# The order of the experts in an attention, expert-routing and two-layer kernel: the two small experts move from the middle to the last step

## The chip, the cores and the metric

The kernel runs on one core of a Trainium2 chip. The metric is the device time of one execution in microseconds, and the median of several executions is quoted. TensorE (PE) does the matrix products, VectorE (DVE) and ScalarE (ACT) the elementwise work, GpSimd (POOL) issues the indirect transfers, SyncE (SP) issues all the others. Each engine works through its own queue in the order in which the program was written. They meet at semaphores.

## The reference, cut to what matters

Three layers follow each other: attention in a window of 64 positions, a layer of eight experts of which each token uses one, and a two-layer network that all tokens use.

```python
def _attn_ref(q, k, v):                      # 2 x 8 heads x 576 positions x 64
    scores = np.where(mask, scale * q @ k.T, -1e9)      # mask: 0 <= i - j < 64
    attn = softmax(scores)
    return attn @ v                          # as x: 1152 tokens x 512

def _moe_ref(x, w_gate, w1, w2, capacity):   # 8 experts, 512 -> 1024 -> 512
    logits = x @ w_gate
    expert_idx = np.argmax(logits, axis=1)
    ...
    h = np.maximum(np.einsum('ecd,edf->ecf', disp, w1), 0.0)
    y = np.einsum('ecf,efd->ecd', h, w2)
    out[i] = gate_w[i] * y[expert_idx[i], pos[i]]

def _moe2_ref(x, w_in, w_out, alpha):        # 512 -> 2048 -> 512
    h = x @ w_in
    g = np.maximum(h, 0.0) + alpha * np.minimum(h, 0.0)
    return g @ w_out
```

How many tokens an expert gets is known only when the router has run. The inputs are of type float32.

## The kernel before, in words

**Attention and routing** take the first 78 us. The experts are then ranked by how many tokens they have, rank 0 the largest. Eight positions p = 0 to 7 follow each other, and the table ORDER says which rank stands at which position. `room` gives each position a size: ranks 1 to 3 are **wide** (256 tokens), ranks 0, 4 and 5 **narrow** (128; the first 128 tokens of rank 0 have been done ahead in the attention phase), and ranks 6 and 7 are the **pair** (64 tokens each). What doesn't fit goes to a rare second pass.

**Weights.** An expert has eight chunks of 512 KB: four of its first matrix, four of its second. `stream` is the order in which the chunks are loaded. SP loads a chunk into a raw slot as soon as one is free (`load_on`, L110). There are 14 slots in this phase; only five of them may hold chunks of the network behind the experts (L115). A chunk of a wide or narrow expert is **split** into a rounded part `whi` (ACT L1017, every fourth on DVE) and the rest `wlo` (DVE L144); the split frees the raw slot and fills one of seven ring places. `prepare` writes these splits into the queues up to seven chunks ahead of the product that uses them. The pair is not split: its products read the raw chunks, which keep their slots until then.

**Products.** A wide expert computes in `wide_up` four times 24 matmuls of 256 columns (tile `hps`, L1033), after each of which ACT and DVE make `hh` (L1041) and `hl` (L1042), and in `wide_down` 96 matmuls (tile `y`, line 220, written by `mm3`) into four accumulators y0 to y3 for the four quarters d of the model's width. `put` turns each of them into the columns `x2h` (ACT L1059) and `x2l` (DVE L1060) that the network reads. A narrow expert does `sps`, `stp`, `sy` likewise, and its result is transposed (`ytp`) inside the next expert, as an entry of the list `late`. `ready` transposes the next expert's tokens (`xtp`, L1008) and splits them into `xwh` and `xwl` (L1093, L1094) for a wide, `xth` and `xtl` for a narrow one.

**The pair** runs as a generator inside the expert at position HOST: `pair()` transposes the pair's tokens, copies them on DVE to `xp` (L1171), and yields; then four times `pps` (L1189) with a yield after each, then four times `py` (L1205). `wide_up` and `wide_down` call it between their own chunks, by `between(c)`. Its result goes through `done` (ytp, then two pairs of ACT L1222 and DVE L1223), again by `late`.

**The network behind the experts** (`second_mlp`) computes `gps` (L220) and `ops` (L1326) in four rounds. Its weights come as 64-bit numbers, and `cvt_tick` makes float32 of them and splits them: per half chunk ACT L166 and L189, DVE L173, L174, L177 and L190. Four ticks stand inside the expert at position 7, which is wide: two in `wide_up` (after c = 2 and c = 3), two in `wide_down`, beside put(0) and put(1). Its first matmuls read all four quarters of x2 one after the other, quarter d in matmuls 3d to 3d + 2.

Before the change ORDER is (0, 1, 4, 5, 2, 6, 7, 3) and HOST is 4: narrow, wide, narrow, narrow, wide with the pair in it, wide.

Of the kernel before, what the change touches and what calls it, by code (L numbers as in the profile page):

```python
# [27 lines left out]
def attention_moe_mlp_kernel(  # L28
# [13 lines left out]
    nc = tc.nc  # L42
    B, S = 2, 576
    NE, NT, D = 8, 1152, 512
# [5 lines left out]

    ORDER = (0, 1, 4, 5, 2, 6, 7, 3)
    HOST, PAIR = 4, (5, 6)
    WIDE, NARROW, HALF = min(cap, 256), 128, 64
    room = [WIDE if 1 <= r <= 3 else HALF if r >= 6 else NARROW for r in ORDER]
    NS = 2 * NE + 1
# [15 lines left out]
    raws, parts = {}, {}  # L73
    n_moe = wmoe.shape[0]

    stream = [(p, c) for p in range(HOST) for c in range(8)]
    stream += [(p, c) for c in range(8) for p in (HOST, *PAIR)]
    stream += [(p, c) for p in range(PAIR[-1] + 1, 8) for c in range(8)]
    split = [n for n, (p, _) in enumerate(stream) if p not in PAIR]
    n_split = len(split)  # L80
    first_part = {p: split.index(stream.index((p, 0))) for p in range(8) if p not in PAIR}
# [49 lines left out]
    def ring_tiles(c):  # L131
        ring = ring_a if c % RING < RING_A else ring_b
        width = 1024 if c % RING < RING_A else 2 * VROOM
        parts[c] = tuple(ring.tile([128, width], F32R, name=x, tag=x)[:, :1024] for x in ("whi", "wlo"))
        return parts[c]
# [26 lines left out]
    def cvt_a(n):  # L162
        if n >= 2 * n_mlp:
            return
        mags[n] = cvt.tile([128, ROW], F32, name="mag", tag="mag")[:, :512]
        nc.scalar.activation(out=mags[n], in_=words(n)[1].bitcast(F32), func=AF.Abs, scale=2.0 ** -111)  # L166
# [14 lines left out]
    def cvt_c(n):  # L181
        if n < 0 or n >= 2 * n_mlp:
            return
        w = words32.pop(n)
        c = n_split + n // 2
        if n % 2 == 0:
            ring_tiles(c)
        hi, lo = (x[:, 512 * (n % 2):512 * (n % 2) + 512] for x in parts[c])
        nc.scalar.copy(hi, w)  # L189
        nc.vector.tensor_tensor(lo, w, hi.bitcast(F32), op=ALU.subtract)  # L190
# [3 lines left out]
    def cvt_tick(free):  # L194

        n = cvt_n[0]
        if n > 2 * n_mlp or n_split + n // 2 - RING > free:
            return
        if n == 0:
            cvt_a(0)  # L200
        cvt_c(n - 1)
        cvt_a(n + 1)
        cvt_b(n)
        cvt_n[0] += 1
# [17 lines left out]
    with tc.manual_schedule():  # L222
        identf = const.tile([128, 128], F32, name="identf")
        gt = const.tile([128, NTILE, 8], F32, name="gt")
        tok = const.tile([128, NTILE], I32, name="tok")
# [10 lines left out]
        with ExitStack() as es:  # L236
# [537 lines left out]
            def sort():  # L774
# [12 lines left out]
                for r0 in range(0, NE, 2):  # L787
                    p0, p1 = ORDER.index(r0), ORDER.index(r0 + 1)
                    nc.vector.tensor_scalar(keyp[:, p0:p1 + 1:p1 - p0], top[:, r0:r0 + 2], 64.0, None, op0=ALU.mult)
# [132 lines left out]
            for c in (2, 3):  # L922
                pe_ahead((c,))
                cs = slice(2 * c - 4, 2 * c - 2)
# [40 lines left out]
        with ExitStack() as es:  # L965
# [47 lines left out]
            def prepare(used):  # L1013

                c = ahead[0]
                if c < n_split and split[c] in raws and c < used + RING and (c > 7 or used > 2):
                    (nc.vector.tensor_copy if c % 4 == 3 else nc.scalar.copy)(ring_tiles(c)[0], raws[split[c]])  # L1017
                    prep_lo(c, nc.vector)
                    ahead[0] += 1

            late = []

            def wide_up(p, xt, between=lambda c: None):
                hT, at = [], first_part[p]
                for c in range(4):
                    hi, lo = (w.rearrange("p (k f) -> p k f", k=4) for w in parts.pop(at + c))
                    ps = ps_h.tile([128, 2, WIDE], F32, name="hps", tag="h")
                    for f in range(2):
                        fs = slice(128 * f, 128 * f + 128)

                        for n, (i, j) in enumerate(((0, 0), (1, 0), (0, 1))):
                            for kk in range(4):
                                nc.tensor.matmul(ps[:, f, :], (hi, lo)[i][:, kk, fs], xt[j][:, kk, :],  # L1033
                                                 start=n == kk == 0, stop=n == 2 and kk == 3)
                        while late and f:
                            late.pop(0)()
                        if f == 0:
                            prepare(at + c)
                    hh = hp.tile([128, 2, WIDE], F32R, name="hh", tag="hh")
                    hl = hp.tile([128, 2, WIDE], F32R, name="hl", tag="hl")  # L1040
                    nc.scalar.activation(out=hh, in_=ps, func=AF.Relu)  # L1041
                    nc.vector.scalar_tensor_tensor(hl, ps, 0.0, hh.bitcast(F32), op0=ALU.max, op1=ALU.subtract)  # L1042
                    hT.append((hh, hl))
                    between(c)
                    prepare(at + c + 1)
                    if p == NE - 1:
                        cvt_tick(at + c - 1)
                return hT

            def wide_down(p, win, hT, between=lambda c: None):  # L1050
                at = first_part[p] + 4
                ys = [ps_y.tile([128, WIDE], F32, name=f"y{d}", tag="y") for d in range(4)]

                def part(c, f, d, hi, lo):
                    dd = slice(128 * d, 128 * d + 128)
                    mm3(ys[d], (hi[:, f, dd], lo[:, f, dd]), [x[:, f, :] for x in hT[c]], c == 0 and f == 0, c == 3 and f == 1)

                def put(d):
                    nc.scalar.copy(x2[0][:, d, win], ys[d])  # L1059
                    nc.vector.tensor_tensor(x2[1][:, d, win], ys[d], x2[0][:, d, win].bitcast(F32), op=ALU.subtract)  # L1060

                if p == NE - 1:
                    w2 = [[w.rearrange("p (k f) -> p k f", k=2) for w in parts.pop(at + c)] for c in range(4)]
                    for ds, cs in (((0, 1), (0, 1, 2)), ((0,), (3,)), ((1,), (3,)), ((2,), range(4)), ((3,), range(4))):
                        for d in ds:
                            for c in cs:
                                for f in range(2):
                                    part(c, f, d, *w2[c])
                            if 3 in cs:
                                put(d)  # L1070
                                if d < 2:
                                    cvt_tick(at - 1)
                    return
                for c in range(4):
                    hi, lo = (w.rearrange("p (k f) -> p k f", k=2) for w in parts.pop(at + c))
                    for f in range(2):
                        for d in range(4):
                            part(c, f, d, hi, lo)
                        prepare(at + c)
                    between(c)  # L1080
                for d in range(4):
                    put(d)
                prepare(at + 4)
# [144 lines left out]
            wins, xts = {}, {}  # L1228
# [10 lines left out]
            def ready(p):  # L1239
                if p == PAIR[0]:  # L1240
                    p = PAIR[-1] + 1
                if p < NE:
                    wins[p] = window(1 + p, room[p], compute[1:])
                    xts[p] = halves_of(p)
# [8 lines left out]
            for p in range(1, NE):  # L1253
                if p == HOST:
                    two = pair()
                    next(two)
                    hT = wide_up(p, xts.pop(p), lambda c: next(two))
                    ready(p + 1)
                    wide_down(p, wins[p], hT, lambda c: next(two))
                    next(two, None)  # L1260
                elif p in PAIR:
                    continue
                elif room[p] == WIDE:
                    hT = wide_up(p, xts.pop(p), lambda c: gather_gates() if (p, c) == (1, 1) else None)
                    if p == NE - 1:
                        nc.vector.tensor_copy(tok, gt[:, :, 0])
                    ready(p + 1)
                    wide_down(p, wins[p], hT)
                else:
                    narrow(p, wins[p], xts.pop(p))  # L1270
# [97 lines left out]
        with tc.If(n_over > 0, preferred_fallthrough_block=True):  # L1368
# [3 lines left out]
            with ExitStack() as es:  # L1372
# [3 lines left out]
                for j in range(NTILE):  # L1376
# [7 lines left out]
                    cs = slice(128 * j, 128 * j + 128)  # L1384
# [15 lines left out]
            for p in range(NE):  # L1400
# [5 lines left out]
                with tc.If(here > 0), ExitStack() as es:  # L1406
# [6 lines left out]
                    at = nc.values_load(inci[0:1, NS + p:NS + p + 1], engines=(mybir.EngineType.SP,),  # L1413
                                        min_val=0, max_val=n_moe - 8)
# [84 lines left out]
```

## Time and profile before

| | us |
|---|---|
| median of 3 executions | 417.22 (415.33 to 417.91) |
| the profiled execution, its own time | 418.03 |
| its span, first to last instruction | 416.3 |
| PE busy in the span | 396.3 (95%) |
| mean granted clock of PE | 0.98 |
| attention, routing, work ahead | 0 to 78.2 |
| the experts, positions 0 to 7 | 78.2 to 208.7 |
| the network behind them | 208.7 to 406.8 |

Times in the trace are counted from the start of the span. A row of the timeline has its start, its duration and, in brackets, how long the engine stood idle before it and what ended that. The chain of waits runs back from the last instruction, at each step to what released it; a wait that it names cost PE something only where PE stood idle as well, and that has to be looked up in PE's own timeline. "Busy" of PE counts pipelined matmuls from issue to their modelled end, so short delays between matmuls are hidden in it; they show in the length of a stretch when it is set beside an equal one.

### The profile page before, as it was taken

The numbers are of one execution on the slowest core, as the hardware profiler recorded it, in microseconds if no ns is written. First come the engines' busy times: TensorE is split into PE (matmuls) and PEld (weight loads), VectorE is DVE, ScalarE is ACT, GpSimd is POOL, SyncE is SP. The second block draws the span as 40 slices with busy tenths as digits, with TensorE's granted clock in tenths as the row PEclk, the third lists the DMA queues.
The fourth block names the chain that finished last, engine by engine and source line by source line (L and its number), as shares of the span: only waits on it lengthen the run. The fifth ranks groups of instructions, "written<-read, shape, count | busy, mean of one in ns | idle before, by whom it ended". The sixth has DMA issues, their size and how long they took to land.

```text
span 416.3 us, 7856 instructions
## 1 busy us (share of the span) xinstructions
PE 396.3 (95%) x2925; PEld 351.4 (84%) x2925; DVE 285.4 (69%) x676; ACT 198.2 (48%) x371; POOL 58.2 (14%) x125
## 2 busy tenths in 40 slices
PE   6999789999999998999999999999999999999990
PEld 4888588789999876779999988998899988999880
DVE  2788567688997854536779966999949982356220
ACT  3788415567376453333457655676307720255000
POOL 4721236310000560000000000000000000000431
PEclk9999869999999999999999999999999999999997
DMA  7920953999988899731423243333411000000221
GB/s 265 371 59 8 351 231 129 333 411 401 313 290 284 248 306 323 272 97 46 153 86 118 101 153 112 142 111 141 140 64 54 0 2 0 0 2 1 78 101 56
DMA packets 20447, 66.13 MB, mean 159 GB/s; under 512 B 2992, under 2 KB 2992, under 8 KB 20400
## 3 DMA queue, kind: packets, MB, share of 16 engines
q1 hardware_dynamic: 17872, 58.00, 39.9%
q0 software_dynamic: 2528, 7.53, 5.0%
q8 instruction: 25, 0.41, 0.4%
q14 instruction: 22, 0.18, 0.1%
HBM read 60.74 MB, written 4.79 MB: 157 GB/s over the span
## 4 chain that ended last, share of the span: by engine, by line
PE 87%; DVE 5%; DMA 3%; ACT 2%; issue 2%; POOLq 0%; ACTq 0%; POOL 0%; DVEq 0%
PE gps L220 24%; PE ops L1326 24%; PE y L220 8%; PE hps L1033 6%; PE sps L220 3%; PE sy L220 3%; DMA raw<-moe_in 3%; PE sc L406 3%; PE av L448 2%; PE tp L434 2%; PE py L1205 2%; PE aps L745 2%; PE ay L756 2%; PE tx L464 1%; PE xap L689 1%
## 5 line engine op out<-in xcount | busy, mean ns | idle before, releaser
L144 DVE TENSOR_TENSOR wlo<-raw,whi 128x1024 fp32r<-128x1024 f32 x45 | 54.2, 1223 | 19.2 <-ACT whi L1017 13.7
L220 PE MATMUL gps<-x2h,wlo 128*128 128x384 f32 x192 | 64.2, 334 | 0.0
L220 PE MATMUL gps<-x2h,whi 128*128 128x384 f32 x192 | 64.2, 334 | 0.0
L220 PE MATMUL gps<-x2l,whi 128*128 128x384 f32 x192 | 64.2, 334 | 0.0
L1326 PE MATMUL ops<-whi,gl 128*128 128x512 f32 x144 | 56.1, 390 | 0.0
L1326 PE MATMUL ops<-wlo,gh 128*128 128x512 f32 x144 | 56.1, 390 | 0.0
L1326 PE MATMUL ops<-whi,gh 128*128 128x512 f32 x144 | 56.0, 389 | 0.0
L1302 ACT ACTIVATE u<-gps,one 128x384 f32<-128x384 f32 x48 | 27.7, 577 | 55.0 <-PE gps L220 55.0
L1334 POOL DMA_INDIRECT out<-acc,tok x9 | 8.7, 965 | 245.9 <-ACTq L1368 233.1
L1303 DVE SCALAR_TENSOR_TENSOR g<-gps,slope,u 128x384 f32<-128x384 f32 x48 | 29.4, 613 | 18.9 <-ACT u L1302 18.8
L1332 DVE SCALAR_TENSOR_TENSOR acc<-ops,gate,acc 128x512 f32<-128x512 f32 x27 | 19.9, 748 | 30.7 <-PE ops L1326 30.7
L1017 ACT CAST whi<-raw 128x1024 fp32r<-128x1024 f32 x30 | 31.0, 1049 | 16.6 <-PE y L220 11.9
L220 PEld LDWEIGHTS gps<-x2l,whi 128*128 128x128 f32 x192 | 36.0, 188 | 0.1
L220 PEld LDWEIGHTS gps<-x2h,whi 128*128 128x128 f32 x192 | 36.0, 188 | 0.1
L220 PEld LDWEIGHTS gps<-x2h,wlo 128*128 128x128 f32 x192 | 36.0, 188 | 0.0
L1313 ACT ACTIVATE gh<-g,sign 128x384 fp32r<-128x384 f32 x48 | 29.3, 611 | 9.5 <-DVE g L1303 9.5
L1326 PEld LDWEIGHTS ops<-whi,gl 128*128 128x128 f32 x144 | 27.0, 188 | 5.6
L1326 PEld LDWEIGHTS ops<-wlo,gh 128*128 128x128 f32 x144 | 27.0, 188 | 5.6
L1326 PEld LDWEIGHTS ops<-whi,gh 128*128 128x128 f32 x144 | 27.0, 188 | 5.5
L1314 DVE SCALAR_TENSOR_TENSOR gl<-g,sign,gh 128x384 fp32r<-128x384 f32 x48 | 29.2, 609 | 0.2 <-ACT gh L1313 0.2
L220 PE MATMUL y<-hh,whi 128*128 128x256 f32 x96 | 27.7, 288 | 1.6 <-ACT spht L1196 1.6
L190 DVE TENSOR_TENSOR wlo<-w,whi 128x512 fp32r<-128x512 f32 x32 | 21.9, 686 | 7.9 <-ACT whi L189 7.8
(267 smaller groups left out, 816.5 us busy)
## 6 DMA issues: line engine op xcount, KB each, us to landing
raw<-moe_in SPq DMA_DIRECT2D x61, 512.0 KB, 4.9
raw<-mlp_in SPq DMA_DIRECT2D x32, 512.0 KB, 3.3
v<-v_in SPq DMA_DIRECT2D x8, 260.0 KB
sw<-moe_in SPq DMA_DIRECT2D x4, 512.0 KB, 11.4
qT<-q_in SPq DMA_DIRECT2D x6, 256.0 KB
kT<-k_in SPq DMA_DIRECT2D x6, 256.0 KB, 5.9
qT<-q_in SPq DMA_DIRECT2D x2, 384.0 KB
kT<-k_in SPq DMA_DIRECT2D x2, 384.0 KB, 5.5
```

The source lines that it names most:

```text
L144: eng.tensor_tensor(lo, raws.pop(split[c]), hi.bitcast(F32), op=ALU.subtract)
L190: nc.vector.tensor_tensor(lo, w, hi.bitcast(F32), op=ALU.subtract)
L220: nc.tensor.matmul(ps, wa[i], xa[j], start=start and n == 0, stop=stop and n == 2)
L406: nc.tensor.matmul(sc[s][64 * e:64 * e + 64, p, :], qT[b][h, i, p, :], kT[b][h, w:w + 2, p, :])
L1017: (nc.vector.tensor_copy if c % 4 == 3 else nc.scalar.copy)(ring_tiles(c)[0], raws[split[c]])
L1033: nc.tensor.matmul(ps[:, f, :], (hi, lo)[i][:, kk, fs], xt[j][:, kk, :], start=n == kk == 0, stop=n == 2 and kk == 3)
L1302: nc.scalar.activation(out=u, in_=ps, func=AF.Copy, scale=one[:, ft:ft + 1])
L1303: nc.vector.scalar_tensor_tensor(g, ps, slope[:, ft:ft + 1], u, op0=ALU.mult, op1=ALU.max)
L1313: nc.scalar.activation(out=gh, in_=g, func=AF.Copy, scale=sg)
L1314: nc.vector.scalar_tensor_tensor(gl, g, sg, gh.bitcast(F32), op0=ALU.mult, op1=ALU.subtract)
L1326: nc.tensor.matmul(ps, a_[:, ts_], b_[:, f % 2, :], start=f == 0 and n == 0, stop=f == 3 and n == 2)
L1332: nc.vector.scalar_tensor_tensor(acc[:, tt, :], ps, sc, acc[:, tt, :], op0=ALU.mult, op1=ALU.add)
```

## The change

The second wide expert moves ahead of the second narrow one, and the pair moves from position 4's expert into the last wide one, at position 7. The positions are now narrow, wide, narrow, wide, narrow, and a wide one with the pair. The weights' stream follows: positions 0 to 4 one after the other, then chunk by chunk of the pair and of position 7 in turn. The pair's generator is advanced twice before `wide_up`, so that its `pps` for chunk 0 stands ahead of the host's first product, and each later step stands one step earlier as well. In the last `wide_down` quarters 0 and 1 take chunks 0 to 2 with the pair's `py` between them, then chunk 3; then come the pair's transposes and conversions (`late.pop`), put(0), put(1) with their ticks, and quarters 2 and 3 as before.

```diff
-    ORDER = (0, 1, 4, 5, 2, 6, 7, 3)
-    HOST, PAIR = 4, (5, 6)
+    ORDER = (0, 1, 4, 2, 5, 6, 7, 3)
+    HOST, PAIR = 7, (5, 6)
...
-    stream = [(p, c) for p in range(HOST) for c in range(8)]
-    stream += [(p, c) for c in range(8) for p in (HOST, *PAIR)]
-    stream += [(p, c) for p in range(PAIR[-1] + 1, 8) for c in range(8)]
+    stream = [(p, c) for p in range(PAIR[0]) for c in range(8)]
+    stream += [(p, c) for c in range(8) for p in (*PAIR, HOST)]
...
-                if p == NE - 1:
-                    w2 = [[w.rearrange("p (k f) -> p k f", k=2) for w in parts.pop(at + c)] for c in range(4)]
-                    for ds, cs in (((0, 1), (0, 1, 2)), ((0,), (3,)), ((1,), (3,)), ((2,), range(4)), ((3,), range(4))):
-                        for d in ds:
-                            for c in cs:
-                                for f in range(2):
-                                    part(c, f, d, *w2[c])
-                            if 3 in cs:
-                                put(d)
-                                if d < 2:
-                                    cvt_tick(at - 1)
+                if p == HOST:
+                    w2 = []
+                    for c in range(3):
+                        w2.append([w.rearrange("p (k f) -> p k f", k=2) for w in parts.pop(at + c)])
+                        for f in range(2):
+                            for d in range(2):
+                                part(c, f, d, *w2[c])
+                            prepare(at - 1)
+                        between(c)
+                    between(3)
+                    w2.append([w.rearrange("p (k f) -> p k f", k=2) for w in parts.pop(at + 3)])
+                    for d in range(4):
+                        for c in range(3 if d < 2 else 0, 4):
+                            for f in range(2):
+                                part(c, f, d, *w2[c])
+                        if d == 0:
+                            continue
+                        if d == 1:
+                            late.pop(0)()
+                            put(0)
+                            cvt_tick(at - 1)
+                        put(d)
+                        if d == 1:
+                            cvt_tick(at - 1)
                     return
...
                 if p == HOST:
                     two = pair()
                     next(two)
+                    next(two)
                     hT = wide_up(p, xts.pop(p), lambda c: next(two))
-                    ready(p + 1)
-                    wide_down(p, wins[p], hT, lambda c: next(two))
-                    next(two, None)
+                    nc.vector.tensor_copy(tok, gt[:, :, 0])
+                    wide_down(p, wins[p], hT, lambda c: next(two, None))
```

Three places in the queues matter below. A row is an instruction (or several equal ones) with its line, its operation, what it writes and reads, and the size.

**PE, where the pair begins.** Before, at the end of position 3:

```order
L220 MATMUL sy<-whi,sl__2373 128x512
L1008 MATMUL xtp<-identf,xg 128x128 x4
L1033 MATMUL hps<-xwh,whi 128x256 x4
L1033 MATMUL hps<-xwh,wlo 128x256 x4
L1033 MATMUL hps<-xwl,whi 128x256 x4
L1033 MATMUL hps<-xwh,whi 128x256 x4
L1033 MATMUL hps<-xwh,wlo 128x256 x4
L1033 MATMUL hps<-xwl,whi 128x256 x4
L1135 MATMUL ytp<-identf,spysb 128x128 x4
L1189 MATMUL pps<-raw,xp 64x256 x8
```

Now, at the end of position 4:

```order
L219 MATMUL sy<-whi,sl__2694 128x512
L1007 MATMUL xtp<-identf,xg 128x128 x4
L1201 MATMUL pps<-raw,xp 64x256 x8
L1032 MATMUL hps<-xwh,whi 128x256 x4
L1032 MATMUL hps<-xwh,wlo 128x256 x4
```

The 24 matmuls `hps` and the four of `ytp` that stood between the transposes of the pair's tokens (`xtp`) and the first use of their copy `xp` now stand behind that use.

**DVE, at the same place: what stands ahead of the copy to `xp`.** Before:

```order
L1120 TENSOR_TENSOR sl__2373<-stp,sh 128x512
L962 TENSOR_LOAD inci
L1094 TENSOR_TENSOR xwl<-xtp,xwh 128x4x128 x2
L144 TENSOR_TENSOR wlo<-raw,whi 128x1024 x2
L962 TENSOR_LOAD inci x2
L1171 COPY xp<-xtp 128x512
```

Now:

```order
L1132 TENSOR_TENSOR sl__2694<-stp,sh 128x512
L961 TENSOR_LOAD inci
L1106 TENSOR_TENSOR xwl<-xtp,xwh 128x4x128 x2
L1016 CAST whi<-raw 128x1024
L143 TENSOR_TENSOR wlo<-raw,whi 128x1024 x2
L961 TENSOR_LOAD inci x2
L1183 COPY xp<-xtp 128x512
```

One CAST of a weight chunk more stands ahead of the copy.

**DVE, at the end of the last expert.** Before, from the copy of the token numbers to the first conversion of the network's words:

```order
L1266 CAST tok<-gt 128x9
L1060 ISA
L1060 TENSOR_TENSOR x2l<-y_3043,x2h 128x256
L190 TENSOR_TENSOR wlo<-w,whi 128x512
L173 TENSOR_SCALAR w<-raw 128x512
L174 SCALAR_TENSOR_TENSOR w<-raw,w 128x512
L177 SCALAR_TENSOR_TENSOR w<-mag,w 128x512
```

Now:

```order
L1271 CAST tok<-gt 128x9
L1235 ISA
L1235 TENSOR_TENSOR x2l<-ytp,x2h 128x4x64
L1235 ISA
L1235 TENSOR_TENSOR x2l<-ytp,x2h 128x4x64
L1059 ISA
L1059 TENSOR_TENSOR x2l<-y_3016,x2h 128x256
L189 TENSOR_TENSOR wlo<-w,whi 128x512
L172 TENSOR_SCALAR w<-raw 128x512
L173 SCALAR_TENSOR_TENSOR w<-raw,w 128x512
L176 SCALAR_TENSOR_TENSOR w<-mag,w 128x512
```

The two conversions of the pair's result, which stood in the middle of position 7's `wide_up`, now stand ahead of the put of quarter 0 (`y_3016`), and with it of all that follows.

## Rows read from the trace of the kernel before

**Rows 1.** The page: busy time, share of span and instructions of the engines.

```profile
PE 396.3 (95%) x2925; PEld 351.4 (84%) x2925; DVE 285.4 (69%) x676; ACT 198.2 (48%) x371; POOL 58.2 (14%) x125
```

**Rows 2.** The chain of waits, whole run: start us, duration us, what.

```profile
104.00 11.51 PE y L220 x96
115.51 4.24 PE sps L220 x36
128.03 2.84 PE sps L220 x24
139.15 2.78 PE sy L220 x12
142.37 2.83 PE hps L1033 x24
150.11 6.27 DMA raw<-moe_in
158.39 5.80 DMA raw<-moe_in
168.40 1.87 PE py L1205 x8
185.44 3.03 PE hps L1033 x24
188.47 0.44 PE ytp L1220 x4
208.76 24.96 PE gps L220 x144
```

**Rows 3.** PE's timeline, 163 to 169 us: start, duration, instruction, idle before.

```profile
166.35 0.39 PE L220 MATMUL y<-hh,whi 128*128 128x256 f32 x1 [1.65 <-ACT spht L1196]
```

**Rows 4.** PE by tile, 142.3 to 185.5 us: busy us, mean ns, idle before.

```profile
L1189 PE MATMUL pps<-raw,xp 128*64 128x256 f32 x64 | 7.8, 385 | 0.0
```

**Rows 5.** DVE's timeline, 138.9 to 143.7 us.

```profile
139.01 1.49 DVE L1094 TENSOR_TENSOR xwl<-xtp,xwh 128x512 fp32r<-128x512 f32 x2 [0.57 <-ACT xwh L1093]
140.75 2.36 DVE L144 TENSOR_TENSOR wlo<-raw,whi 128x1024 fp32r<-128x1024 f32 x2 [0.26 <-ACT whi L1017]
143.03 0.68 DVE L1171 COPY xp<-xtp 128x512 f32<-128x512 f32 x1
143.63 0.69 DVE L1017 CAST whi<-raw 128x1024 fp32r<-128x1024 f32 x1
```

**Rows 6.** PE's timeline at 8 us, at 46 us, and at 208.5 us.

```profile
8.20 0.48 PE L406 MATMUL sc<-kT,qT 64*64 64x128 f32 x2 [1.83 <-DVE nm L419]
...
46.47 0.34 PE L448 MATMUL av<-v,ptT 128*64 128x65 f32 x4 [2.13 <-ACT ptT L440]
...
208.60 0.34 PE L220 MATMUL gps<-x2h,whi 128*128 128x384 f32 x1
```

**Rows 7.** Stretches: length, busy of PE, PEld, DVE, ACT, POOL, clock, DMA share, GB/s.

```profile
48.30:58.60 10.30, 9.76 (x93) 8.49 (x93) 6.01 (x35) 3.29 (x9) 1.11 (x3) 0.50 0.76 307
142.30:185.40 43.10, 41.45 (x310) 31.34 (x308) 23.02 (x28) 16.65 (x25) 9.09 (x8) 1.00 0.75 258
164.70:166.40 1.70, 0.05 (x2) 0.05 (x1) 1.05 (x1) 1.70 (x4) 0.00 (x0) 1.00 0.79 263
208.70:406.80 198.10, 198.06 (x1009) 180.73 (x1007) 138.89 (x243) 89.62 (x162) 8.43 (x16) 1.00 0.21 74
```

**Rows 8.** DVE's timeline, 202 to 210 us: the end of position 7.

```profile
202.72 0.42 DVE L1060 TENSOR_TENSOR x2l<-y,x2h 128x256 f32 x1 [1.65 <-ACT x2h L1059]
205.64 0.42 DVE L1060 TENSOR_TENSOR x2l<-y,x2h 128x256 f32 x1
208.81 0.82 DVE L1060 TENSOR_TENSOR x2l<-y,x2h 128x256 f32 x2
```

**Rows 9.** The first and last conversion of the pair's result: ACT's and DVE's timelines, 188 to 191 us.

```profile
188.95 0.38 ACT L1222 CAST x2h<-ytp 128x256 f32 x1 [2.81 <-PE ytp L1220]
190.22 0.42 DVE L1223 TENSOR_TENSOR x2l<-ytp,x2h 128x256 f32 x1 [0.44 <-ACT x2h L1222]
```

**Rows 10.** Weight loads, by tile: time from issue to landing, whole run and 142 to 170 us.

```profile
DMA to landing us min/median/max: 3.2/4.5/12.3
DMA to landing us min/median/max: 4.4/5.0/5.6
```

More of the change, by code (lines that the diff above doesn't have):

```diff
@@ L1060, in put @@
                     nc.vector.tensor_tensor(x2[1][:, d, win], ys[d], x2[0][:, d, win].bitcast(F32), op=ALU.subtract)
-                if p == NE - 1:
-                    w2 = [[w.rearrange("p (k f) -> p k f", k=2) for w in parts.pop(at + c)] for c in range(4)]
-                    for ds, cs in (((0, 1), (0, 1, 2)), ((0,), (3,)), ((1,), (3,)), ((2,), range(4)), ((3,), range(4))):
-                        for d in ds:
-                            for c in cs:
-                                for f in range(2):
-                                    part(c, f, d, *w2[c])
-                            if 3 in cs:
-                                put(d)
-                                if d < 2:
-                                    cvt_tick(at - 1)
+                if p == HOST:
+                    w2 = []
[21 more added lines that the diff above has]
+                            cvt_tick(at - 1)
                     return
@@ L1264, in attention_moe_mlp_kernel @@
                     hT = wide_up(p, xts.pop(p), lambda c: gather_gates() if (p, c) == (1, 1) else None)
-                    if p == NE - 1:
-                        nc.vector.tensor_copy(tok, gt[:, :, 0])
                     ready(p + 1)
```

## The prediction

> **What bounds the kernel now.** I read four views in this order: the page, the chain of waits, PE's timeline, and the stretches. The page has PE busy for 95% of the span [rows 1], and from 208.7 us on it is busy for 198.06 of 198.10 us [rows 7]: the network behind the experts is bound by PE alone, and the change doesn't touch it. What can move is the stretch of the experts, 78.2 to 208.7 us. There the chain of waits names two transfers of weights, 6.27 and 5.80 us long [rows 2], inside the expert that hosts the pair. Read alone, that promises 12 us. But PE's own timeline shows how much of it PE felt: between 142.3 and 185.4 us it is busy for 41.45 of 43.10 us [rows 7], with one gap of 1.65 us at 164.7 us [rows 3]. The transfers were late for ACT and DVE, and PE had other work almost all the time.
>
> Busy time can hide small delays, so I also set the stretches beside the work in them, which the chain's starts give [rows 2]. Position 2 (narrow) lasts from 115.51 to 128.03, 12.52 us. Position 3 is also narrow and lasts to 142.37, 14.34 us; it has three sets of four transposes more (0.44 us each, as `ytp`), so 13.84 us are accounted for and **0.50 us are lost**. The host with its pair lasts from 142.37 to 185.44, 43.07 us. Its work: four `hps` of 2.83, `y` 11.51, four `py` of 1.87, five sets of transposes of 0.44 [rows 2], `pps` 7.8 [rows 4]; together 40.31. **Lost: 2.76 us**, the gap of 1.65 and 1.1 more, spread over the stretch. So if the new order cured every delay among the experts, it would give 3.3 us, 0.8% of the time.
>
> **The change part by part.** *Matmuls.* Their number and shapes are the same, and so is the number of changes between split and unsplit products (eight each way), so the 1.1 us spread over the host's stretch I leave where they are: no gain, no loss. Bounds: they may all go (-1.1), or the shorter turns of 12 `y` matmuls may double them (+1.1).
>
> *The loads.* A narrow expert eats eight chunks in 12.5 us, a wide one eight in 23. Before, two narrow ones and the host with its 24 chunks stood in a row; now a wide one stands between the two narrow ones, and the pair's 16 chunks are read last. The two late transfers and the 0.50 us of position 3, where two narrow experts met, should go: **-1.65 and -0.50**. The 24 interleaved chunks all pass through SP's one queue, with the network's first words behind them. Two added waits come of that, and both are covered. First, DVE's CAST of the host's last chunk waits for a load that is issued only when the second `pps` has freed a slot. Behind it on DVE stands `hl` of the host's second product, for which the fourth `hps` waits. Between lie two `hps`, two `pps` (7.8 / 4 = 1.95 each) and a set of transposes: 2 x 2.83 + 2 x 1.95 + 0.44 = 10.0 us of PE. DVE needs a load of up to 5.6 us in the host's stretch before [rows 10], then 0.69, 1.18 and about 0.7 us [rows 5]: 8.2. Second, ACT waits for the network's second words, whose load is issued when the fourth `pps` is done; that is a rival below. Without such cover each late microsecond costs one. POOL's nine gathers of the gates wait for the last gather of tokens, which now finds its buffer free one expert earlier; nobody reads them before the last expert, so I cost them at nothing.
>
> *The pair a step ahead.* Before, 24 `hps` and a set of transposes stood between the transposes of the pair's tokens and the first `pps`, and DVE's copy to `xp` hid behind them. Now `pps` follows at once. Before, PE was through with the transposes at 142.37 [rows 2] and DVE had `xp` ready at 143.03 + 0.68 = 143.71, after two `xwl` and two `wlo` [rows 5]. Now one CAST more, 0.69 us, stands in that queue: 144.40. PE stands idle for 144.40 - 142.37, **+2.0 us**. Bounds: 0.7, the copy alone, if DVE's queue is empty by then; 3.2, if one of the two `wlo` (1.18) starts late by its own length. I take the middle because position 4 now follows a wide expert, so DVE should come neither late nor idle.
>
> This is also where a rule speaks against the change. What the rows show: the gap of 1.65 us at 164.7 left the clock at 1.00, the full 2.4 GHz [rows 3, 7], and one of 1.83 us at 8 us did so too; the gap of 2.13 us that ends at 46.47 [rows 6] was followed by 10.3 us at 0.50, 1.2 GHz [rows 7]. The Trainium skill, page "TensorE: Matmul & The Clock Gate", section "HAM oscillation — how this bites in real kernels", says that a kernel whose TensorE waits between short bursts of matmuls falls back to the slow clock and begins each burst slow. By that rule my sum would be that of the second rival below; by the two shorter gaps it stands.
>
> *The end of the last expert.* Before, the pair's result was converted in the middle of position 7. Now this stands ahead of put(0), in a chain of ACT and DVE in turn. Count from T, where y1's last matmul has been issued. Before, 48 matmuls of y2 and y3 at 11.51 / 96 = 0.12 us follow, and `gps` starts at 208.60 [rows 6], so T = 202.84. DVE started `x2l` of y0 at 202.72 and finished that of y2 half way through the 0.82 us from 208.81, at 209.22 [rows 8], 6.5 us later; that is T + 6.38. `gps` needs it at its eighth matmul, 7 x 24.96 / 144 = 1.21 us after its start, at T + 6.97, so 0.6 us were to spare. Now: `ytp` to T + 0.44; the conversions take 188.95 to 190.64, 1.69 us [rows 9]; put(0) passes ACT first, 0.38; so `x2l` of y0 starts at T + 2.5 and that of y2 is done at T + 9.0. PE needs it at T + 0.44 + 5.76 + 1.21 = T + 7.4: **+1.6 us** of waiting. Bounds: 1.0, if the two ticks between them run 0.6 us closer; 3.0, if ACT comes late to the first conversion by as long as the conversions take. The same two gaps of this size stand against the rule on the clock, and PE is already issuing `gps` when this one comes.
>
> **Sum:** 2.0 + 1.6 - 1.65 - 0.50 = +1.45 us on the profiled execution (418.03 to about 419.5, its span 416.3 to 417.8). The median of the runs shown lies 0.8 us below that execution, so **418.7 us**. The waits that go were hidden for the most part; the two that come stand on PE's path with nothing beside them.
>
> **The rivals.** *Faster, by a little (0.20).* Both new waits come at their lower ends and the whole loss of the host goes: 0.7 + 1.0 - 2.76 - 0.50 = -1.6, **415.7 us**. For it: with the late transfers gone, DVE has more room. Against: the two waits follow from the order in the queues, not from a transfer.
>
> *Slower by the clock (0.08).* One of the two new gaps is long enough for the granted clock to fall to 0.50. Price: in the 10.3 us at that clock PE was busy for 9.76 [rows 7], and half of that, 4.9, is the loss: **423.6 us**. It decides between a gap of 1.83 us, which was borne, and one of 2.13, which was not [rows 6]; my 2.0 lies between. Against: just ahead of the gap at 46 us PE did short matmuls with gaps of their own, whereas here it runs dense on either side, as around 164.7. That favours no fall.
>
> *Slower by the network's words (0.05).* ACT reads the second half chunk's words right after the fourth `pps` has let SP load them, and the copy of the pair's second hidden half, which the third `py` needs, stands behind them. PE meanwhile has `hps` 2.83, two `py` of 1.87, two turns of `y` of 11.51 / 8, and transposes 0.44: 9.9 us. ACT needs the load, 4.5 to 5.6 us, and three passes of some 0.53 us (198.2 / 371 [rows 1]), 7.2 at most. It decides at a load of 8.3 us; the slowest in the trace, 12.3 [rows 10], came when eight were in flight at the start of the experts, and costs 4.0: **422.7 us**.
>
> That the change does nothing of what it says is no rival: the queues show the order moved.
>
> **How the numbers follow.** The forecast has 0.65, and 0.02 remain for what I have not seen. The range runs from the faster rival's end, 415.7, to the forecast with both waits at their upper ends: 3.2 + 3.0 - 2.15 = +4.05, 421.3; with a few tenths for the spread of the medians, **415.4 to 421.6**. That leaves out the two slower rivals. A measurement of this kernel can tell about 1%, 4.2 us, from no change. Faster than 413.0 would take more than the 3.3 us that there are to win: 0.02. Slower than 421.4: the two slower rivals, and the forecast's upper end: 0.15. Within 1%: 0.83.
>
> **What would show it.** In the changed kernel's trace: no idle PE and no named transfer in positions 2 to 4, and position 4 without the 0.50 us; a gap of about 2 us before the first `pps`, released by DVE's `xp`; the host's `hps` and `y` running on without a wait for a transfer; a gap of about 1.6 us within the first twelve `gps`, released by DVE's `x2l`; the clock at 1.00 throughout. It is wrong if DVE is so far ahead that the first `pps` finds its copy, if ACT's wait for the network's words reaches PE, or if positions 2 to 4 get shorter by more than 0.5 us: then the split of the weights had been costing more than PE's gaps show.

## The result and the profile after

The changed kernel takes **420.24 us** (median of 11 runs, 418.71 to 423.89) against 417.22 before (11 runs, 415.2 to 418.7). The medians lie 3.0 us apart, the means 3.9, and the ratio is **1.0094 [1.0070, 1.0117]**. The forecast was 418.7, in a range up to 421.6, with "within 1%" as the likeliest case. The time lies in the range and the case holds, though the interval of the ratio reaches past 1%; and a loss forecast as 1.45 us came out at more than twice that.

The profiled execution of the changed kernel took 422.61 us, its span 420.9. Two places of TensorE's (PE's) timeline hold the two waits that were forecast: the first `pps` behind the transposes of the pair's tokens, and the first `gps` of the network (start, duration, instruction, idle time before it and what ended that).

```profile
166.27 0.60 PE L1007 MATMUL xtp<-identf,xg 128*128 128x128 f32 x4
168.77 3.57 PE L1201 MATMUL pps<-raw,xp 128*64 128x256 f32 x16 [1.90 <-DVE xp L1183]
172.27 0.74 PE L1032 MATMUL hps<-xwh,whi 128*128 128x256 f32 x4
...
180.55 1.95 PE L1201 MATMUL pps<-raw,xp 128*64 128x256 f32 x16
...
185.84 1.95 PE L1201 MATMUL pps<-raw,xp 128*64 128x256 f32 x16
187.72 0.74 PE L1032 MATMUL hps<-xwh,whi 128*128 128x256 f32 x4
...
214.34 0.45 PE L219 MATMUL gps<-x2l,whi 128*128 128x384 f32 x1 [1.57 <-DVE x2l L1059]
```

The gaps are 1.90 and 1.57 us, and each is ended by the copy and the subtraction that the prediction named. A third thing stands in the same rows: the first 16 `pps` last 3.57 us, later sets of the same 16 last 1.95. The stretches say why (length, then busy time of PE, PEld, DVE, ACT and POOL, the granted clock, the share of the DMA engines, GB/s):

```profile
166.90:168.80 1.90, 0.03 (x2) 0.03 (x2) 1.82 (x3) 0.15 (x1) 0.00 (x0) 1.00 0.41 119
168.80:172.40 3.60, 3.60 (x17) 1.77 (x18) 1.00 (x1) 1.04 (x1) 0.00 (x0) 0.53 0.69 229
172.40:211.80 39.40, 39.40 (x292) 30.45 (x293) 15.22 (x26) 12.49 (x23) 0.00 (x0) 1.00 0.48 165
```

Right behind the gap the granted clock is about half (0.50 in the clock's records from 168.93 to 172.34, 3.41 us): 1.2 GHz instead of 2.4. In 3.41 us PE did what takes half of that, so this cost **1.7 us**. The last row shows the other side: for 39.4 us, through the whole host with its pair, PE is never idle, where the kernel before had its gap of 1.65 us [rows 3].

The VectorE (DVE) rows ahead of the first `pps` are the queue that the prediction counted through: two `xwl`, a CAST, two `wlo`, and only then the copy to `xp`.

```profile
163.83 1.29 DVE L1106 TENSOR_TENSOR xwl<-xtp,xwh 128x512 fp32r<-128x512 f32 x2 [0.89 <-ACT xwh L1105]
165.04 0.68 DVE L1016 CAST whi<-raw 128x1024 fp32r<-128x1024 f32 x1
165.75 2.36 DVE L143 TENSOR_TENSOR wlo<-raw,whi 128x1024 fp32r<-128x1024 f32 x2
168.03 0.69 DVE L1183 COPY xp<-xtp 128x512 f32<-128x512 f32 x1
```

A sum by stages closes the account. I count from the first `sps`, with which the experts begin (the texts of the experiments call it the first score product), since the work ahead of it is the same in all kernels. From there to the end of the span it is 416.3 - 77.7 = 338.6 us before and 420.9 - 78.4 = 342.5 after: **+3.9**. The two gaps give 1.90 + 1.57, the half clock 1.69 (3.57 less the 1.88 of the next set of 16 in the chain); so -1.3 is left for all that the new order cured, where the forecast had -2.15.

One place gave some back. Position 3 is now wide, and by the chain's starts takes 24.15 us (129.25 to 153.40) where position 1, wide as well, takes 23.71 (92.52 to 116.23): +0.44. The chain of waits there (start, duration, what) shows DVE busy with the splits of the next weights while `hl`, which the next `hps` needs, stands behind them:

```profile
134.61 1.23 DVE wlo L143
135.83 0.60 DVE whi L1016
136.44 0.03 issue
136.47 0.04 DVE wlo L143
136.51 1.11 issue
137.62 0.69 DVE hl L1041
138.31 0.04 issue
138.35 3.10 PE hps L1032 x24
```

### The profile page after: what moved, and what is told of

Its sections match the earlier page's. It is cut to its first block, busy times and chain, and to the rows that moved or that the text cites. A ratio compares the mean times of both kernels' runs of the same rounds, so it can differ in the third digit from the quotient of the medians.

```text
span 420.9 us, 7856 instructions
## 1 busy us (share of the span) xinstructions
PE 395.9 (94%) x2925; PEld 349.5 (83%) x2925; DVE 285.1 (68%) x676; ACT 198.1 (47%) x371; POOL 57.2 (14%) x125
## 4 chain that ended last, share of the span: by engine, by line
PE 88%; DVE 6%; issue 2%; ACT 1%; another core or an unknown queue 1%; DVEq 0%; POOLq 0%; POOL 0%
PE gps L219 24%; PE ops L1336 23%; PE y L219 7%; PE hps L1032 7%; PE sps L219 4%; PE sy L219 3%; PE sc L405 2%; PE pps L1201 2%; PE tp L433 2%; PE aps L744 2%; PE av L447 2%; PE py L1217 2%; PE ay L755 2%; DVE ms L418 1%; PE tx L463 1%
```

## The experiments

The first four ran on one chip, with the kernel before at 417.8 us there (19 runs); the next three on a second, where it took 409.9 (20 runs); the last three on a third, where it took 410.24 (17 runs). Ratios are always to the runs of before on the same chip.

**The first gap alone.** The pair's tokens are transposed and copied within position 4, ahead of the last two weight splits:

```
-                prepare(at + 5)
-                second(2)
+                if p + 1 == PAIR[0]:
+                    second(2)
+                    begun.append(pair())
+                    next(begun[0])
+                    prepare(at + 5)
+                else:
+                    ...
```

> The changed kernel with one thing moved: the pair's tokens are transposed and copied to xp inside position 4, between its third and fourth quarter of sy, ahead of the last two weight splits on DVE. Theory (the loss is the two gaps of 1.90 and 1.57 us plus the slow clock that follows the first one, 1.7 us): the gap ahead of the first pps and the slow clock behind it are both gone, the gap at the first gps of 1.6 us stays; 420.2 - 1.9 - 1.7 = 416.6 us. Rival (the new order of experts and loads is itself slower, and the gap only shows waiting that would come elsewhere): the gap goes, another wait of about its size appears in position 7, and the time stays at 419.5 to 420.5. Second rival (the clock falls for another reason than the gap): gap gone, clock still at 0.5 for 3.4 us near the start of position 7, 418.3 us.

Measured: 419.95 us, ratio 1.0048 [1.0025, 1.0071]. The first gap is gone: `xp` is copied at 165.19, and `pps` follows `sy` at once.

```profile
165.19 0.69 DVE L1189 COPY xp<-xtp 128x512 f32<-128x512 f32 x1 [0.39 <-PE xtp L1007]
165.80 0.68 DVE L1016 CAST whi<-raw 128x1024 fp32r<-128x1024 f32 x1
166.51 2.36 DVE L143 TENSOR_TENSOR wlo<-raw,whi 128x1024 fp32r<-128x1024 f32 x2
```

But the time fell by less than the gap and its half clock together, and stayed where the first rival had put it. That rival's sign, another wait of about the gap's size in position 7, is not there: the largest new one is 0.31 us. PE's rows at the first `gps` show where the clock went: the second gap is the same 1.58 us, and now it is this one that is followed by half clock, from 212.23 to 215.64.

```profile
210.90 0.44 PE L219 MATMUL gps<-x2l,whi 128*128 128x384 f32 x1 [1.58 <-DVE x2l L1059]
...
212.05 0.36 PE L219 MATMUL gps<-x2l,whi 128*128 128x384 f32 x1
212.22 0.51 PE L219 MATMUL gps<-x2h,wlo 128*128 128x384 f32 x1
212.53 0.52 PE L219 MATMUL gps<-x2h,whi 128*128 128x384 f32 x1
```

**The step ahead undone.** The new order, with the first `pps` behind the first `hps` again:

```
-                    next(two)
-                    hT = wide_up(p, xts.pop(p), lambda c: next(two))
+                    hT = wide_up(p, xts.pop(p), lambda c: [next(two) for _ in range(1 if c else 2)])
```

> The changed kernel with the head of the pair's lead undone: the first pps stands behind the host's first hps again, followed at once by the second pps; all later steps stand as in the changed kernel. Theory: the copy to xp hides behind the hps, no gap and no slow clock: 420.2 - 1.9 - 1.7 = 416.6 us, and the gap of 1.6 us at the first gps stays. Rival (the new order itself is slower): 419.5 to 420.5 us.

Measured: 423.47 us, ratio 1.0127 [1.0092, 1.0162], no faster than the change as a whole. The first gap is gone here too, but another has come, ahead of the fourth `hps`. In PE's row and the chain of waits:

```profile
187.29 0.74 PE L1032 MATMUL hps<-xwh,whi 128*128 128x256 f32 x4 [1.69 <-DVE hl L1041]
```

```profile
171.81 3.65 PE pps L1201 x32
...
176.52 8.14 DMA raw<-moe_in
184.66 0.02 issue
184.69 0.71 DVE whi L1016
...
186.56 0.70 DVE hl L1041
```

This is the first of the two "covered waits" of the prediction. PE's cover is as long as the prediction had it: from the end of the second `pps` (171.81 + 3.65 = 175.46) to where the fourth `hps` could have begun (187.29 - 1.69 = 185.60) are 10.1 us. The load is what doesn't hold. The `pps` come later and in one block, SP issues six loads within 7.0 us (10.4 in the changed kernel), and the last takes 8.14 us, where the chain of waits in the host's stretch before had 6.27 at most [rows 2]. The CAST that waits for it holds `hl` back. So undoing the step moves the first gap and doesn't remove it. That this version is slower than the changed kernel is not shown: the two intervals overlap, and in the profile the part from the first `sps` takes 421.84 - 80.08 = 341.8 us, 0.8 less than in the changed kernel, with half clock for 3.41 us behind the gap of 1.58 us at `gps`.

**The second gap alone.** The second of the two ticks that split the network's words stands behind the last `put` instead of the second one:

```
-                        if d == 1:
+                        if d == 3:
                             cvt_tick(at - 1)
```

> The changed kernel with the second conversion step of the network's words (the tick beside put(1)) moved behind put(3). Theory: x2l of quarters 2 and 3 no longer waits for it, the gap of 1.57 us within the first gps goes, 420.2 - 1.6 = 418.6 us; the gap ahead of the first pps and the slow clock behind it stay as they are. Rival (DVE is short of time there anyway): the moved step delays the first g and u of the network or its second chunk of weights, a wait of 1 to 2 us appears in the first gps round, and the time stays at 420.

Measured: 420.9 us, ratio 1.0062 [1.0032, 1.0091]. There is no idle PE at `gps`, and the part from the first `sps` takes 419.3 - 79.0 = 340.3 us, 2.2 less than in the changed kernel (1.57 of it is the gap; the rest is not placed). The first gap, 1.92 us, and half clock behind it stay:

```profile
169.39 3.42 PE L1201 MATMUL pps<-raw,xp 128*64 128x256 f32 x16 [1.92 <-DVE xp L1183]
```

```profile
169.70:173.10 3.40, 3.40 (x17) 1.70 (x14) 1.16 (x1) 1.04 (x1) 0.00 (x0) 0.50 0.61 217
```

**PE kept busy in the first gap**, with 16 matmuls whose result nobody reads, so that the wait is the same and only the idleness goes:

```
+                ones = identf.bitcast(BF16)
+                idle = ps_x.tile([128, 512], F32, name="idle2", tag="x")[:, :256]
+                for _ in range(16):
+                    nc.tensor.matmul(idle, ones[:, :128], ones, start=True, stop=True)
```

> The changed kernel with 16 extra matmuls of 256 columns (bfloat16, a constant against itself, result never read) between the transposes of the pair's tokens and the first pps: some 1.7 us of work for PE in the gap, nothing else changed. It tells the gap from the clock. Theory (the clock falls because PE stands idle): the first pps starts when it did, since it still waits for xp, but the clock stays at 1.00 and the eight pairs of pps take 1.9 instead of 3.57 us: 420.2 - 1.7 = 418.5 us. Rival (the clock falls for another reason, for instance that the sparse pps draw little): the slow clock stays, 420.2 us. Had the extra matmuls lengthened the stretch, 420.5.

Measured: 423.4 us, ratio 1.0128 [1.0102, 1.0154]. In the trace it did what it was to do: the wait stands, and the `pps` behind it take 1.95 us at full clock.

```profile
169.37 0.60 PE L1007 MATMUL xtp<-identf,xg 128*128 128x128 f32 x4
169.80 1.91 PE L1187 MATMUL idle<-identf 128*128 128x256 bf16 x16
171.89 1.95 PE L1205 MATMUL pps<-raw,xp 128*64 128x256 f32 x16 [0.17 <-DVE xp L1183]
```

That fits idle time, and not the wait as such, as what brings half clock; by itself it doesn't show it, since the unfilled gap too was spared half clock in one profile of three (the changed kernel's second, below). Yet the whole time was higher, because the work ahead of the experts took 81.5 us in this execution, 3.1 more than in the changed kernel, with two stretches at half clock:

```profile
46.80:53.70 6.90, 6.90 (x92) 6.20 (x88) 4.33 (x23) 3.84 (x12) 0.00 (x0) 0.51 1.00 407
63.90:70.70 6.80, 6.16 (x15) 4.84 (x16) 1.30 (x1) 1.96 (x4) 3.98 (x5) 0.50 0.45 108
```

Whether the filling had a part in that, this run could not say; so it was run again below.

**Both gaps at once**: the first and the third edit together.

> The changed kernel with both edits that took one of its two gaps each: the copy to xp stands within position 4, and the second tick of the two row tiles stands behind the last x2l. Theory (the change costs two gaps of TensorE, 1.90 and 1.57 us, and 1.69 us of half clock behind the first): no gap over 0.5 us before the first pps and none within the first gps, clock 1.00 from the first score product on, and the stretch from there to the end of the span 342.5 - 1.9 - 1.6 - 1.7 = 337.3 us, against 338.6 in the kernel before; time 415 to 417, ratio 0.994 to 1.000. Rival (the copy and the tick only hand the wait on to the next stage's weights or to the splits): gaps of over 1 us show up elsewhere, stretch 339 or more, ratio 1.002 to 1.006. Rival (the time goes by the clock in attention, not by the gaps): stretch 337 to 338 and yet a time of 418 or more.

Measured: 409.85 us against 409.9, ratio **1.0006 [0.9993, 1.0019]**. The part from the first `sps` takes 408.6 - 70.9 = 337.7 us, where 337.3 was expected. From there to PE's last matmuls at 398.2 us PE is idle for 327.30 - 326.85 = 0.45 us in all, no gap is above 0.25 us, and the clock is at 1.00:

```profile
70.90:398.20 327.30, 326.85 (x1985) 295.40 (x1984) 232.80 (x379) 152.97 (x258) 26.05 (x31) 1.00 0.43 152
```

**The step ahead alone**, in the order before: a second `next(two)` ahead of the host's `wide_up`.

> The kernel before with its order of the experts, and only the step ahead added: a second tick of the pair of small experts where the first one stands, so that the first pps stands ahead of its host. Theory (the step ahead brings the gap before the first pps, whatever the order): a gap of 1.4 to 2.2 us there, released by VectorE's xp, the clock's fall behind it or not, and the gap within the host (1.65 us in the kernel before) gone or smaller; 0 to +2.5 us, ratio 1.000 to 1.006. Rival (the order brings it: a wide expert before the host leaves VectorE later than a narrow one does): no gap over 0.7 us before the first pps, and the time 415.5 to 417, ratio 0.996 to 1.000.

Measured: 411.5 us, ratio 1.0034 [1.0019, 1.0049], from the first `sps` 410.1 - 71.1 = 339.0 us. The gap comes with the step, in the old order as well, 0.5 us shorter than in the new one, and without half clock; the gap within the host is gone:

```profile
135.18 0.60 PE L1008 MATMUL xtp<-identf,xg 128*128 128x128 f32 x4
137.21 1.95 PE L1189 MATMUL pps<-raw,xp 128*64 128x256 f32 x16 [1.43 <-DVE xp L1171]
139.09 0.74 PE L1033 MATMUL hps<-xwh,whi 128*128 128x256 f32 x4
```

**The changed kernel once more**, beside these two.

> The changed kernel as it is, once more, beside the two others. Theory: the gaps of 1.9 and 1.6 us stand again in the same two places, since the order of instructions sets them; half clock behind one of them at least, for about 3.4 us; ratio 1.007 to 1.012, stretch from the first score product 341 to 343 us. Rival (the clock's fall was that one execution's): gaps as before, no half clock behind either, stretch 340.5 to 341, and a median no more than 1.007 of the kernel before.

Measured: 414.8 us, ratio 1.0107 [1.0084, 1.0129], from the first `sps` 413.4 - 71.0 = 342.4 us. Both gaps stand where they stood, but half clock has changed sides: none behind the first gap, 3.41 us of it (205.55 to 208.96) behind the second.

```profile
161.35 1.95 PE L1201 MATMUL pps<-raw,xp 128*64 128x256 f32 x16 [1.93 <-DVE xp L1183]
...
205.28 0.47 PE L219 MATMUL gps<-x2l,whi 128*128 128x384 f32 x1 [1.57 <-DVE x2l L1059]
205.56 0.51 PE L219 MATMUL gps<-x2h,wlo 128*128 128x384 f32 x1
```

**The kernel before once more**, for a second profile.

> The kernel before as it is, for a second profile. Theory: one gap of about 1.65 us within the host and one or two of 0.1 to 0.5 us, stretch from the first score product 337.5 to 338.7 us, with no half clock behind the gap; only the stretch ahead of it (77.7 us in the first profile) varies, from 70.5 to 80. Rival (half clock follows this gap as it follows those of the changed kernel): about 3.4 us at half clock behind it and a stretch of 340 or more.

Measured: 410.56 us, one run; from the first `sps` 408.8 - 70.9 = 337.9 us. The gap within the host is there, but it is 0.69 us and not 1.65 [rows 3]:

```profile
158.50 0.38 PE L220 MATMUL y<-hh,whi 128*128 128x256 f32 x1 [0.69 <-ACT spht L1196]
```

So the loss that the new order was to cure varies between executions, since loads set it; the two waits that it brings are 1.90 to 1.93 and 1.57 to 1.58 us wherever they were seen.

**The filling once more.**

> The changed kernel with the filling matmuls in its first gap, once more, since the first time the stretch ahead of all changes took 81.5 us. Theory (the filling itself costs nothing and saves the half clock; the high time came from attention's clock): the part from the first score product takes 340.7 to 341 us when the second gap is without half clock and 342.5 with it, and the time is at or under the changed kernel's, ratio 1.005 to 1.011. Rival (the filling costs time wherever it runs): ratio 1.012 to 1.016, as the first time.

Measured: 413.57 us, ratio 1.0081 [1.0054, 1.0108], from the first `sps` 412.0 - 70.9 = 341.1 us, 1.3 less than the changed kernel. In this profile the work ahead took 70.9 us, as in the kernel before (70.9), and the clock behind the filled gap is at 1.00 again, so here the filling slowed nothing. The first profile has its excess ahead of the experts, where the clock was low; whether all six runs of that measurement had it there, and why, stays open.

**The old order with step ahead and early copy**: the step-ahead kernel with the first experiment's edit in the narrow position ahead of its host.

> The kernel before in its old order, with the step ahead and with the copy to xp within the narrow position ahead of the host, as in the other early copies. Theory (the step ahead pays once VectorE's copy is out of TensorE's way, and the order of the experts does not matter for it): the gap of 1.43 us ahead of the first pps goes, the host's own gap of 1.65 us stays away, so that the stretch from the first score product to the end of the span comes to 339.0 - 1.4 = 337.6 us against 338.6 in the kernel before; ratio 0.995 to 0.999. Rival (the early copy delays the splits of the host's first chunk): a gap of over 0.8 us before the first or second hps, ratio 1.001 to 1.004.

Measured: **409.76 us** against 410.24, ratio **0.9982 [0.9967, 0.9998]**; from the first `sps` 408.0 - 70.4 = 337.6 us. `xp` is copied while PE still does `sy`, and the `pps` follow:

```profile
134.74 0.40 PE L220 MATMUL sy<-whi,sl__2373 128*128 128x512 f32 x1
135.06 1.95 PE L1195 MATMUL pps<-raw,xp 128*64 128x256 f32 x16
136.94 0.74 PE L1033 MATMUL hps<-xwh,whi 128*128 128x256 f32 x4
```

This is the only version with an interval below 1. It is faster than the kernel before by some 0.7 us, barely, and faster than the changed one by about 1.2% if the two ratios are set side by side (0.9982 against 1.0107, measured on two chips).

## Why the prediction was right, and where its size was off

**What bounds the kernel.** Right. The network behind the experts didn't move but for the gap at its start, and the two named transfers of before [rows 2] were no 12 us to be won: the version of the new order that has no gap left equals the kernel before.

**The loads, -1.65 and -0.50.** Mis-sized. Both losses did go. No transfer reached PE in the host, and position 4 takes 13.31 us (153.40 to 166.71, 0.44 after its last transposes begin), where the narrow position's 12.52 and two sets of transposes more make 13.40. But position 3 gave 0.44 us back, and in the sum by stages only 1.3 us is left; the 0.4 us between that and 1.65 + 0.50 - 0.44 = 1.71 is not placed. There was also less to win than 3.3 us: the new order with both gaps removed takes 337.7 us from the first `sps`, 0.9 and 0.2 less than the two profiles of the kernel before. The prediction also took one execution's gap for the kernel's: in the second profile it was 0.69 us, and against that one the changed kernel's second profile is 342.4 - 337.9 = 4.5 us longer, which is 1.93 + 1.57 + 1.7 - 0.7. The prediction left the 1.1 us spread over the host where they are, and nothing showed that they moved.

**The pair a step ahead, +2.0.** Right: 1.90 and 1.93, by the queue that was counted. That it stands on PE's path is shown by the early copy, which removes it, and that the step makes it and not the order, by the step alone (1.43 us).

**The end of the last expert, +1.6.** Right: 1.57 and 1.58 us wherever the tick stands, none where it is moved.

**The covered waits.** Right for the kernel as changed. The load that the CAST waited for landed at about 183.0, and PE had work until 187.7, where the fourth `hps` began without a gap; ACT's wait for the network's words reached PE nowhere. How thin the first margin was, the second experiment showed: with a load of 8.14 us it became a gap of 1.69.

**The clock.** This is the step that failed, and most of the error in size. "It decides between a gap of 1.83 us, which was borne, and one of 2.13, which was not", the prediction said, gave the rival 0.08, and had "the clock at 1.00 throughout" among its signs. Length doesn't decide it here, and the first of the two gaps was misread. In the profiles of all these kernels there are twelve gaps of 1.43 to 1.93 us among the experts and at `gps`, and behind five of them the clock fell: behind 1.90 in the changed kernel but not behind its 1.57; behind 1.57 but not behind 1.93 when it ran again; behind 1.58 in two experiments and 1.92 in a third, and not behind 1.43, 1.65, 1.69 or 1.57 in others. No profile shows it behind two of them.

As for the gap of 1.83 us at 8 us, the prediction read that the clock stayed at 1.00 behind it. But that profile's clock records begin at 14.19 us, and a view of a stretch shows 1.00 where there is no record. PE's own rows tell what the clock was: the same eight transposes take 1.97 us in the kernel before and 1.09 in the version with the step ahead undone, whose records have the full clock there. The kernel before, then that version:

```profile
10.35 1.97 PE L434 MATMUL tp<-identf,pt 128*128 128x128 f32 x8
```

```profile
9.48 1.09 PE L433 MATMUL tp<-identf,pt 128*128 128x128 f32 x8
```

So in the kernel before PE was still at 1.2 GHz, and that gap could not show what the clock bears. In seven of the other profiles, whose records have the full clock ahead of this gap (1.82 to 1.84 us), 3.41 us at half clock begin 0.8 to 1.5 us behind it; in an eighth, the one with the step ahead undone, the records begin within the gap and no fall follows. The changed kernel's rows:

```profile
7.64 1.69 PE L405 MATMUL sc<-kT,qT 64*64 64x128 f32 x32 [1.84 <-DVE nm L418]
```

```profile
5.10:8.50 3.40, 1.56 (x49) 1.32 (x47) 1.78 (x16) 2.19 (x8) 0.82 (x3) 1.00 1.03 342
8.50:11.90 3.40, 3.40 (x38) 2.74 (x31) 1.85 (x16) 1.48 (x4) 2.98 (x12) 0.50 1.04 409
```

Nor does a fall need one long gap: in the first experiment's profile half clock begins at 48.39 us, as it did behind the gap of 2.13 us in the kernel before, though PE's only gaps over 0.3 us from 43 us on are four of 0.38 to 0.69.

The price was mis-sized the other way, 4.9 us from a stretch of 10.3 [rows 7]: each of the five lasted 3.41 us, with PE busy all the while, and so cost about 1.7. With two gaps and, by the count of five in twelve that came later, about a 0.4 chance each, 1.45 + 2 x 0.4 x 1.7 = 2.8 would have been the better sum.

The Trainium skill, page "TensorE: Matmul & The Clock Gate", section "HAM oscillation — how this bites in real kernels", describes a kernel whose waits are longer than its short bursts of matmuls, and says that each burst then begins at the slow clock. This kernel's case among the experts is another: TensorE is dense around the gaps (39.4 us without idle time soon after the first one), and half clock still followed five of twelve.

All five falls between the first `sps` and the end of PE's work come 0.2 to 1.3 us after such a gap, none comes elsewhere, and the two versions without a gap of over 0.3 us have none. So the gaps bring the falls; what picks the five is open.

**The account.** Forecast and measured (from the first profiles): loads -2.15 and -1.3 (what is left over in the sum); step ahead +2.0 and +1.90; end of the last expert +1.6 and +1.57; clock 0 and +1.69; together +1.45 and +3.9. The rest of the difference between the two spans, 0.7 us, lies ahead of the experts and is no part of the change. Removing both gaps, and with them the fall of the clock, brought 1.0107 to 1.0006: those three terms account for the change's loss. That the time stayed in the range is in part luck: the range left the clock's fall out, and its 1.7 us fitted only because the room kept for longer waits was not needed. "Within 1%" is as narrow: the second measurement of the changed kernel has 1.0107.

## What to carry to other kernels

A wait that an engine's queue makes (a copy behind two splits) comes every time and can be priced from rows to a tenth; a late transfer that it replaces may be a matter of one execution, so price a cure by more than one profile. A gap of 1.5 to 2 us on a dense TensorE cost its length here and, in five cases of twelve, 1.7 us more of half clock behind it; add that to the sum with its chance, and look for the order on the releasing engine that avoids the gap. Before a row is taken as proof that the clock bore a gap, look whether the clock had been up ahead of it; the duration of equal matmuls tells. Undoing half of a change can open another wait, as the later `pps` did here.

## What the runs showed of the hardware that was not expected

- The clock's fall behind a short gap among the experts or at `gps` lasts 3.41 us with PE fully busy in it, and comes 0.2 to 1.3 us after the gap's end (five of twelve gaps).
- The same instructions ahead of the experts took 70.4 to 71.1 us in the profiles of two chips and 77.7 to 81.5 in the earlier ones. In all the slower ones there are 6.8 to 13.7 us at half clock between 46 and 71 us, as in the two stretches shown above, and none in the faster ones. The slower ones also have idle time there that the faster ones lack: 2.13 us at 46 us in the kernel before [rows 6], 2.3 to 2.9 us in one gap at 60 to 65 us in four others. The difference is more than the change itself, and it is why the parts from the first `sps` were compared, and runs on the same chip.
